# Six weight shifts moved from PSUM to SBUF, and another order of evictions and stores in the last step, in a fused attention and MoE kernel

## The chip, the cores and the metric

The kernel runs on one core of a Trainium2 chip. A core has five engines with an instruction queue each: TensorE (PE, matrix products into PSUM), VectorE (DVE), ScalarE (ACT), GpSimd (POOL) and SyncE (SP, which here issues every DMA). They run side by side and wait for each other through semaphores. SBUF is the working memory, PSUM the accumulation memory of eight banks that PE writes. The metric is the device time of one execution in microseconds; lower is better.

## The reference, cut to what matters

```python
def _attn_ref(q, k, v):                         # (4, 8, 768, 64)
    k_sum = k.reshape(B, H, nb, 32, D).max(axis=3)
    v_sum = v.reshape(B, H, nb, 32, D).mean(axis=3)
    scores_l = where(|i - j| < 16, scale * q @ k^T, -1e9)
    scores_s = scale * q @ k_sum^T + log(32)
    a = softmax(concat([scores_l, scores_s]))
    return a @ concat([v, v_sum])

def _moe_ref(x, w_in, w_out):                   # 3072 x 512, 512 x 2048, 2048 x 512
    h = x @ w_in
    return (h * cos(h)) @ w_out
```

The result of the attention, with its heads side by side, is the `x` of the second part. Everything is float32.

## The kernel before, in words

**Blocks, groups and steps.** The 3072 rows are done in eight blocks of 384. For each block four groups (a to d, two heads each) compute attention and leave the block's `x`, split into a high and a low part. Then, for each of 16 weight slices of 128 columns of `w_in` and 128 rows of `w_out`, a step forms `h`, its gate and the second product, which adds up in three PSUM banks, one for each chunk of 128 rows. Blocks 0 and 1 share the weights' loading: runs are block 0 with slices 0 to 5, block 1 with all 16, block 0 with slices 6 to 15 (its partial sums lie in DRAM meanwhile), and then blocks 2 to 7. There are 128 steps, `s0` to `s127`.

**The weights.** Each slice `w0` to `w15` is loaded in a raw form and turned into the values that PE multiplies, by a chain of operations on a tile of 128 x 1024: `ab` (`magnitude`, ACT, L388, into SBUF place `stage`), `cl` (`clamp`, L393, DVE or POOL, in place), `sh` (`shift`, DVE, L399), `lb` (`last_bits`, DVE, L407, in place), `fb` (`first_bits`, DVE, L415, into `stage` again), `hi` (copy to the high part, L350 on ACT or L352 on DVE) and `lo` (the rest, L356, on POOL or DVE). Where the shift's result goes is the token's argument: `w1.sh.6.7` is PSUM banks 6 and 7, through `work_in` and `two_banks`; the result also decides what L407 reads and writes and what L415 reads as its second operand, as their first operand is the raw slice in SBUF. The final weights of slice f live in an SBUF tile with the tag `w{f}`; the tiles `w8` to `w15` serve as raw and other room (`late0` to `late7`) before that.

**The order.** Each engine's queue follows one list written out by hand, `ORDER`: a token names who, what and with which arguments (`a0.nm` is the normalisation of group a of block 0; `.a`, `.v`, `.p` at the end is ACT, DVE or POOL). An engine takes its instructions strictly in this order. Around the shifts of slices 0 to 5, POOL has the softmax operations `su` (L593, subtract the maximum) and `nm` (L617, multiply by the inverse sum), the low parts `lo` and one clamp (`w3.cl.p`); DVE has the maxima (L588), sums (L609), inverses (L614) and the low parts of `x` (`xl`, L356) between them; PE the scores (L569), transposes (L626) and the values' product (L670).

**The last step.** `s127` adds the products of chunks 0 and 1 with the high part first (`dh`), then in `dl` the low-part products of chunks 0 and 1 and then all three of chunk 2. Then it evicts: `ta` and `tb` negate a bank into SBUF (`negative`, L806 on ACT, L808 on DVE), `st` and `sb` store. With no place named, `ta` takes the first half of a chunk and `tb` the second (`take_half`), in two halves of one tile, and each half is stored by itself (`store_half`, L830).

Of the kernel before, what the change touches and what calls it, by code (L numbers as in the profile page):

```python
# [10 lines left out]
F32 = mybir.dt.float32  # L11
F32R = mybir.dt.float32r
I32 = mybir.dt.int32
# [15 lines left out]
b0.ck.0.v a0.ck.0.a a0.ks.0 a0.ms.5.6 a0.ck.1.a a0.ks.1 b0.q a0.sc c0.tk.0.7 a0.z.1.a a0.z.0.v w1.l c0.ck.0.a a0.mx  # L29
d0.tk.0.1 c0.ks.0 a0.su c0.tq.0 c0.tk.1.3 d0.q c0.cq.a d0.tk.1.4 c0.ms.6.5 d0.ks.1 a0.ex v0_1.h.p c0.ks.1 c0.ck.1.v  # L30
w0.l d0.ks.0 c0.sc a0.sm c0.v c0.z.1.a v0_0.h.v b0.tq.7 c0.z.0.a b0.ms.0.3 b0.ck.1.a a0.iv v0_0.s.p b0.cq.a v0_1.s.v
d0.ck.0.a b0.sc w1.ab.0 c0.mx c0.m d0.tq.5 b0.z.1.a w1.cl.v c0.su d0.ms.2.1 b0.z.0.a w2.l w1.sh.6.7 d0.cq.a d0.ck.1.a
d0.sc w1.lb a0.nm c0.ex a0.v d0.z.1.a w1.fb.1 a0.tp.0.3 d0.z.0.a a0.tp.1.0 w0.ab.0 a0.m d0.mx w1.hi.a w0.cl.v d0.su
d0.m c0.sm w0.sh.4.5 w5.l w1.lo.p c0.iv w2.ab.0 w0.lb c1.m a0.cp.0.a w2.cl.v c0.nm d0.ex b1.q w0.fb.1 a0.cp.1.a w3.l
a0.va.1 d0.sm w0.hi.a d1.m w2.sh.6.7 w0.lo.p c0.tp.0.2 c1.q d0.iv w5.ab.0 w2.lb b1.tq.3 a1.q a0.xh.a d0.nm c0.tp.1.0
w2.fb.1 c0.cp.0.a d0.v c0.cp.1.a w5.cl.v w2.hi.a c0.va.2 a0.xl w2.lo.p d0.tp.0.6 c0.xh.a w5.sh.4.5 w4.l d0.tp.1.7 a1.m
b0.mx w3.ab.0 a1.tq.0 w5.lb b0.su a1.v a1.cq.a a1.ms.1.0 w5.fb.1 w3.cl.p b0.ex b0.m d0.cp.0.a a1.sc b0.sm b1.cq.a
c1.tq.6 d0.cp.1.a c0.xl a1.z.1.a d0.va.3 b0.iv w3.sh.4.5 b0.nm a1.z.0.a b1.m c1.ms.7.2 d0.xh.a a1.mx c1.cq.a d1.q
w4.ab.0 c1.sc w3.lb a1.su b0.v b0.tp.0.0 w5.hi.a b0.tp.1.1 d0.xl w4.cl.v c1.z.0.a c1.v b0.cp.0.a w4.sh.6.7 c1.z.1.a
b1.ms.3.0 b0.cp.1.a v1_0.l c1.mx a1.ex w8.l w4.lb c1.su b0.va.2 b1.sc a1.sm b0.xh.a w5.lo.p c1.ex d1.tq.1 b0.xl  # L40
b1.z.1.a a2.q a1.iv s0.up.2 w4.fb.0 b1.z.0.a a1.nm w3.fb.1 w4.hi.a a1.tp.0.0 d1.cq.a w4.lo.v w9.l d1.ms.3.6 s0.tu
a1.cp.0.a b1.v c1.sm w8.ab.0 a1.tp.1.7 d1.sc s0.re c1.iv a1.cp.1.a s1.up.4 w8.cl.v c1.nm w10.l s0.si b1.mx d1.v
# [130 lines left out]
s123.hi.a s124.si s123.lo.p s124.sq s124.ga s126.up.3 s124.hi.v s124.lo.v s127.up.4 s126.tu s125.tu s125.re s126.re  # L173
s123.dh s126.si s125.si s123.dl s125.sq s126.sq s124.dh s125.ga s125.hi.v s125.lo.v s124.dl s127.tu s125.dh s127.re
s126.ga s127.si s126.hi.v s127.sq s125.dl s126.lo.v s126.dh s127.ga s127.hi.a s126.dl s127.lo.p s127.dh s127.dl
s127.ta.2.a s127.ta.0.0.v s127.st.2 s127.tb.2.v s127.st.0 s127.ta.1.1.v s127.sb.2 s127.st.1
"""

BLOCK = 32
# [4 lines left out]
def tile_kernel(  # L184
# [20 lines left out]
    nc = tc.nc  # L205

    B, H, S, D = q.shape
    NT, DM = out.shape
    DF = w_in.shape[1]
    P = 128  # L210
# [6 lines left out]
    TB = S // 2  # L217
# [20 lines left out]
    xp = ctx.enter_context(tc.tile_pool(name="xp", bufs=1))  # L238
# [51 lines left out]
    for hh in range(2):  # L290
# [3 lines left out]
            out=rows, in_=rows, pattern=[[0, QC + 1], [1, W]], compare_op=ALU.is_ge,  # L294
# [3 lines left out]
            out=rows, in_=rows, pattern=[[0, QC + 1], [-1, W]], compare_op=ALU.is_ge,  # L298
# [28 lines left out]
    wp = ctx.enter_context(tc.tile_pool(name="wp", bufs=1))  # L327
# [15 lines left out]
    def two_banks(i):  # L343
        return banks[:, i : i + 2, :].rearrange("p b n -> p (b n)").bitcast(I32)
# [13 lines left out]
    def room_for(i):  # L358

        return stage.tile([P, 2 * DM], I32, name=f"stage{i}")  # L360

    class Slice:
# [16 lines left out]
        def work_in(self, where):  # L379
            if not where:  # L380
                return self.u
            return two_banks(where[0]) if len(where) == 2 else room_for(*where)

        def magnitude(self, i):
# [317 lines left out]
    class Step:  # L702
# [106 lines left out]


        def take_half(self, i, h, eng):
            if (i, 0) not in self.o:
                t = xp.tile([P, 2, TB], F32R, name="last", tag="xh0%d" % (self.blk % 2)).rearrange("p c n -> p (c n)")
                self.o[i, 0], self.o[i, 1] = (t[:, n * DM // 2 : (n + 1) * DM // 2].bitcast(F32) for n in range(2))
            self.negative(eng, self.o[i, h], self.acc[i][:, h * DM // 2 : (h + 1) * DM // 2])

        def take_rest(self, i, eng):
# [9 lines left out]

        def store_half(self, i, h):
            r0, c = self.blk * TB + i * P, slice(h * DM // 2, (h + 1) * DM // 2)
            nc.sync.dma_start(out=out[r0 : r0 + P, c], in_=self.o[i, h])  # L830

        def store_rest(self, i):
            self.store_half(i, 1)
# [124 lines left out]
```

## Time and profile before

| | us |
|---|---|
| median of 3 runs | 663.58 |
| the three runs | 661.78, 663.58, 663.86 |
| span of the profiled execution | 660.1 |
| busy in it: PE, DVE, ACT, POOL | 632.6, 449.7, 363.9, 221.8 |
| last instruction of PE ends | 655.1 |

The span goes from the first to the last instruction of one profiled execution; that execution's own total isn't given on the page, and the difference to the median of the runs, some 3.5 us, is what lies around the span. A line of a group reads: source line, engine, operation, what it writes and reads, shapes and count, then busy us, mean ns of one, and the idle time in front of it with what ended it. A line of the timeline reads: start, length, engine, line, operation, and in brackets the idle time in front of it. SPq is SP issuing a DMA. In the tiles' names `banks` is PSUM; `stage`, `late`, `w`, `sc`, `t` and `last` are SBUF.

### The profile page before, as it was taken

To read this page: it belongs to the slowest core of one execution; us is meant where nothing else is said; L and a number is where in the kernel's file an instruction comes from. 1 tells how busy PE (TensorE), PEld (TensorE's weight loads), DVE (VectorE), ACT (ScalarE), POOL (GpSimd) and SP (SyncE) were. 2 spreads that over 40 slices of the span, in tenths; PEclk is the share of its full clock that TensorE was granted. 3 is DMA by queue.
4 is the path that set the end of the run, shared out by engine and by line. 5 is a ranking of instruction groups with operands and counts; after the bars stand their busy time and mean duration, and the time that the engine had idled before them with its cause. 6 is when DMAs were issued, how large, how long until landed. Compare 5 with 4: busy or idle time off the path is not lost.

```text
span 660.1 us, 13282 instructions
## 1 busy us (share of the span) xinstructions
PE 632.6 (96%) x5141; PEld 560.2 (85%) x5141; DVE 449.7 (68%) x798; ACT 363.9 (55%) x640; POOL 221.8 (34%) x219
## 2 busy tenths in 40 slices
PE   6478999999999999999999999999999999999996
PEld 5256889989988998898898899889889989899985
DVE  4887999887855576668797777576876756433344
ACT  2656977776554485437477464356554645444342
POOL 4784896764430342301323411112330212010110
PEclk9869999999999999999999999999999999999999
DMA  9997906544243244525445433424364332000001
GB/s 224 259 271 203 276 15 223 169 109 71 55 122 85 91 124 132 127 59 114 111 107 135 147 98 97 114 43 85 115 163 104 92 94 70 5 1 17 16 17 48
DMA packets 167158, 72.68 MB, mean 110 GB/s; under 512 B 136824, under 2 KB 155832, under 8 KB 167096
## 3 DMA queue, kind: packets, MB, share of 16 engines
q1 hardware_dynamic: 167096, 71.84, 40.9%
q8 instruction: 40, 0.66, 0.4%
q14 instruction: 22, 0.18, 0.1%
HBM read 53.72 MB, written 15.73 MB: 105 GB/s over the span
## 4 chain that ended last, share of the span: by engine, by line
PE 86%; DMA 5%; SPq 3%; POOL 2%; DVE 1%; issue 1%; ACT 1%; DVEq 0%; POOLq 0%; ACTq 0%
PE banks L770 39%; PE banks L714 39%; PE banks L569 4%; PE banks L670 3%; DMA late<-in_moe_w_out_dram 3%; DMA late<-in_v_dram 1%; SPq L456 1%; POOL w L356 1%; DMA late<-in_q_dram 1%; POOL gl L356 1%; SPq L493 1%; POOL stage L393 0%; ACT stage L388 0%; PE banks L556 0%; DVE m L588 0%
## 5 line engine op out<-in xcount | busy, mean ns | idle before, releaser
L714 PE MATMUL banks<-xh,w 128*128 128x384 f32 x1024 | 272.1, 337 | 0.1
L770 PE MATMUL banks<-w,gh 128*128 128x512 f32 x768 | 198.1, 393 | 0.2 <-ACT gh L350 0.2
L714 PEld LDWEIGHTS banks<-xh,w 128*128 128x128 f32 x1024 | 185.9, 188 | 2.8 <-ACT pt L350 0.4
L714 PE MATMUL banks<-xl,w 128*128 128x384 f32 x512 | 171.4, 335 | 0.0
L770 PEld LDWEIGHTS banks<-w,gh 128*128 128x128 f32 x768 | 142.6, 188 | 29.0 <-ACT gh L350 0.5
L724 ACT ACTIVATE t<-banks 128x384 int32<-128x384 f32 x128 | 62.5, 489 | 133.6 <-DVE gl L356 54.9
L356 POOL TENSOR_TENSOR gl<-t,gh 128x384 fp32r<-128x384 f32 x55 | 56.6, 1029 | 221.4 <-ACT gh L350 86.0
L770 PE MATMUL banks<-w,gl 128*128 128x512 f32 x384 | 109.8, 394 | 0.1
L727 DVE SCALAR_TENSOR_TENSOR t<-t,banks 128x384 f32<-128x384 int32 x128 | 70.0, 548 | 56.9 <-ACT t L724 56.2
L732 ACT ACTIVATE t<-t 128x384 f32<-128x384 f32 x128 | 66.7, 523 | 66.3 <-DVE t L727 66.0
L714 PEld LDWEIGHTS banks<-xl,w 128*128 128x128 f32 x512 | 96.1, 188 | 1.6
L739 DVE SCALAR_TENSOR_TENSOR t<-t,banks 128x384 f32<-128x384 f32 x128 | 69.3, 546 | 41.2 <-ACT t L735 41.0
L770 PEld LDWEIGHTS banks<-w,gl 128*128 128x128 f32 x384 | 71.1, 188 | 14.6 <-DVE gl L356 0.2
L593 POOL TENSOR_TENSOR sc<-sc,m 128x720 f32<-128x720 f32 x28 | 40.1, 1431 | 129.2 <-DVE m L588 129.2
L735 ACT ACTIVATE t<-t 128x384 f32<-128x384 f32 x128 | 65.8, 521 | 2.1
L617 POOL TENSOR_TENSOR sc<-sc,r 128x720 f32<-128x720 f32 x28 | 39.5, 1411 | 51.4 <-DVE r L614 50.3
L350 ACT CAST gh<-t 128x384 fp32r<-128x384 f32 x68 | 34.7, 510 | 33.2 <-PE banks L770 16.5
L356 DVE TENSOR_TENSOR gl<-t,gh 128x384 fp32r<-128x384 f32 x73 | 41.7, 572 | 12.6 <-ACT gh L350 6.5
L356 POOL TENSOR_TENSOR w<-stage,w 128x1024 fp32r<-128x1024 f32 x15 | 36.2, 2416 | 10.0 <-ACT w L350 8.6
L352 DVE CAST gh<-t 128x384 fp32r<-128x384 f32 x60 | 23.2, 386 | 22.2 <-PE banks L770 20.4
L580 DVE SCALAR_TENSOR_TENSOR sc<-banks,mask 128x360 f32<-128x360 f32 x48 | 24.4, 524 | 19.2 <-PE banks L569 19.0
L569 PEld LDWEIGHTS banks<-kd,qd 64*64 64x64 f32 x1344 | 28.4, 135 | 9.4 <-issue 6.7
(102 smaller groups left out, 620.7 us busy)
## 6 DMA issues: line engine op xcount, KB each, us to landing
pd<-stage SPq DMA_DIRECT2D x22, 384.0 KB
late<-in_moe_w_in_dram SPq DMA_DIRECT2D x16, 512.0 KB
late<-in_moe_w_out_dram SPq DMA_DIRECT2D x16, 512.0 KB
pt<-pd SPq DMA_DIRECT2D x66, 96.0 KB
vn<-in_v_dram SPq DMA_DIRECT2D x52, 120.0 KB
out_dram<-stage SPq DMA_DIRECT2D x23, 256.0 KB
kn<-in_v_dram SPq DMA_DIRECT2D x24, 192.0 KB
qn<-in_q_dram SPq DMA_DIRECT2D x92, 48.0 KB
```

The costliest lines, as they stand in the source:

```text
L350: eng.copy(out=out, in_=in_)
L356: eng.tensor_tensor(out=lo, in0=src, in1=hi.bitcast(F32), op=ALU.subtract)
L569: nc.tensor.matmul(out=self.sp[hh][s * QT : (s + 1) * QT, c, lo : lo + n], lhsT=self.qd[rows, t * QT : (t + 1) * QT], rhs=self.kd[rows, ke ...
L593: nc.gpsimd.tensor_tensor(out=self.sc, in0=self.sc, in1=self.m.unsqueeze(2).broadcast_to([P, U, NK]), op=ALU.subtract)
L617: nc.gpsimd.tensor_tensor(out=self.sc, in0=self.sc, in1=self.r.unsqueeze(2).broadcast_to([P, U, NK]), op=ALU.mult)
L714: nc.tensor.matmul(out=self.h, lhsT=w_of(name, self.f)[:, c * P : (c + 1) * P], rhs=x_of(self.blk, part, c), start=n == 0, stop=n == last,)
L724: nc.scalar.activation(out=self.t.bitcast(I32), in_=self.h, func=AF.Copy, scale=1.0 / TWO_PI)
L727: nc.vector.scalar_tensor_tensor(out=self.t, in0=self.t.bitcast(I32), scalar=-TWO_PI, in1=self.h, op0=ALU.mult, op1=ALU.add)
L732: nc.scalar.activation(out=self.t, in_=self.t, func=AF.Sin, scale=0.5)
L735: nc.scalar.activation(out=self.t, in_=self.t, func=AF.Square, scale=math.sqrt(2.0))
L739: nc.vector.scalar_tensor_tensor(out=self.t, in0=self.t, scalar=-1.0, in1=self.h, op0=ALU.add, op1=ALU.mult)
L770: nc.tensor.matmul(out=self.acc[i], lhsT=g[:, i * P : (i + 1) * P], rhs=w_of(name, self.f), start=self.first and n == 0, stop=self.last an ...
```

## The change

In `ORDER` the six tokens `w1.sh.6.7`, `w0.sh.4.5`, `w2.sh.6.7`, `w5.sh.4.5`, `w3.sh.4.5` and `w4.sh.6.7` become `w1.sh.8`, `w0.sh.8`, and so on, at the same places; nothing else in the list moves up to the last line. The argument 8 makes `work_in` take an SBUF tile with the tag of the slice's own final weights. Slices 6 to 15 keep their banks.

The last line of `ORDER` is another: chunk 0 is evicted by DVE and stored, then chunk 1 by ACT (before: by DVE, last) and stored, then chunk 2 in halves, the first by DVE and the second by ACT (before: the first by ACT, the second by DVE, chunk 2 ahead of chunk 1). The halves get tiles of their own, and the second one's store is issued by ACT's queue.

```diff
-d0.ck.0.a ... w2.l w1.sh.6.7 d0.cq.a d0.ck.1.a
+d0.ck.0.a ... w2.l w1.sh.8 d0.cq.a d0.ck.1.a
...
-s127.ta.2.a s127.ta.0.0.v s127.st.2 s127.tb.2.v s127.st.0 s127.ta.1.1.v s127.sb.2 s127.st.1
+s127.ta.0.0.v s127.st.0 s127.ta.1.1.a s127.st.1 s127.ta.2.v s127.tb.2.a s127.st.2 s127.sb.2
...
         def work_in(self, where):
             if not where:
                 return self.u
+            if where == (8,):
+                return wp.tile([P, 4 * DM], I32, name=f"u{self.f}", tag=f"w{self.f}")[:, : 2 * DM]
             return two_banks(where[0]) if len(where) == 2 else room_for(*where)
...
         def take_half(self, i, h, eng):
-            if (i, 0) not in self.o:
-                t = xp.tile([P, 2, TB], F32R, name="last", tag="xh0%d" % (self.blk % 2)).rearrange("p c n -> p (c n)")
-                self.o[i, 0], self.o[i, 1] = (t[:, n * DM // 2 : (n + 1) * DM // 2].bitcast(F32) for n in range(2))
+            t = xp.tile([P, 2, TB], F32R, name="last", tag="x%s0%d" % ("hl"[h], self.blk % 2))
+            self.o[i, h] = t.rearrange("p c n -> p (c n)")[:, : DM // 2].bitcast(F32)
             self.negative(eng, self.o[i, h], self.acc[i][:, h * DM // 2 : (h + 1) * DM // 2])
...
         def store_half(self, i, h):
             r0, c = self.blk * TB + i * P, slice(h * DM // 2, (h + 1) * DM // 2)
-            nc.sync.dma_start(out=out[r0 : r0 + P, c], in_=self.o[i, h])
+            (nc.sync, nc.scalar)[h].dma_start(out=out[r0 : r0 + P, c], in_=self.o[i, h])
```

More of the change, by code (lines that the diff above doesn't have):

```diff
@@ L31 @@
 w0.l d0.ks.0 c0.sc a0.sm c0.v c0.z.1.a v0_0.h.v b0.tq.7 c0.z.0.a b0.ms.0.3 b0.ck.1.a a0.iv v0_0.s.p b0.cq.a v0_1.s.v
-d0.ck.0.a b0.sc w1.ab.0 c0.mx c0.m d0.tq.5 b0.z.1.a w1.cl.v c0.su d0.ms.2.1 b0.z.0.a w2.l w1.sh.6.7 d0.cq.a d0.ck.1.a
+d0.ck.0.a b0.sc w1.ab.0 c0.mx c0.m d0.tq.5 b0.z.1.a w1.cl.v c0.su d0.ms.2.1 b0.z.0.a w2.l w1.sh.8 d0.cq.a d0.ck.1.a
 d0.sc w1.lb a0.nm c0.ex a0.v d0.z.1.a w1.fb.1 a0.tp.0.3 d0.z.0.a a0.tp.1.0 w0.ab.0 a0.m d0.mx w1.hi.a w0.cl.v d0.su
-d0.m c0.sm w0.sh.4.5 w5.l w1.lo.p c0.iv w2.ab.0 w0.lb c1.m a0.cp.0.a w2.cl.v c0.nm d0.ex b1.q w0.fb.1 a0.cp.1.a w3.l
-a0.va.1 d0.sm w0.hi.a d1.m w2.sh.6.7 w0.lo.p c0.tp.0.2 c1.q d0.iv w5.ab.0 w2.lb b1.tq.3 a1.q a0.xh.a d0.nm c0.tp.1.0
-w2.fb.1 c0.cp.0.a d0.v c0.cp.1.a w5.cl.v w2.hi.a c0.va.2 a0.xl w2.lo.p d0.tp.0.6 c0.xh.a w5.sh.4.5 w4.l d0.tp.1.7 a1.m
+d0.m c0.sm w0.sh.8 w5.l w1.lo.p c0.iv w2.ab.0 w0.lb c1.m a0.cp.0.a w2.cl.v c0.nm d0.ex b1.q w0.fb.1 a0.cp.1.a w3.l
+a0.va.1 d0.sm w0.hi.a d1.m w2.sh.8 w0.lo.p c0.tp.0.2 c1.q d0.iv w5.ab.0 w2.lb b1.tq.3 a1.q a0.xh.a d0.nm c0.tp.1.0
+w2.fb.1 c0.cp.0.a d0.v c0.cp.1.a w5.cl.v w2.hi.a c0.va.2 a0.xl w2.lo.p d0.tp.0.6 c0.xh.a w5.sh.8 w4.l d0.tp.1.7 a1.m
 b0.mx w3.ab.0 a1.tq.0 w5.lb b0.su a1.v a1.cq.a a1.ms.1.0 w5.fb.1 w3.cl.p b0.ex b0.m d0.cp.0.a a1.sc b0.sm b1.cq.a
-c1.tq.6 d0.cp.1.a c0.xl a1.z.1.a d0.va.3 b0.iv w3.sh.4.5 b0.nm a1.z.0.a b1.m c1.ms.7.2 d0.xh.a a1.mx c1.cq.a d1.q
-w4.ab.0 c1.sc w3.lb a1.su b0.v b0.tp.0.0 w5.hi.a b0.tp.1.1 d0.xl w4.cl.v c1.z.0.a c1.v b0.cp.0.a w4.sh.6.7 c1.z.1.a
+c1.tq.6 d0.cp.1.a c0.xl a1.z.1.a d0.va.3 b0.iv w3.sh.8 b0.nm a1.z.0.a b1.m c1.ms.7.2 d0.xh.a a1.mx c1.cq.a d1.q
+w4.ab.0 c1.sc w3.lb a1.su b0.v b0.tp.0.0 w5.hi.a b0.tp.1.1 d0.xl w4.cl.v c1.z.0.a c1.v b0.cp.0.a w4.sh.8 c1.z.1.a
 b1.ms.3.0 b0.cp.1.a v1_0.l c1.mx a1.ex w8.l w4.lb c1.su b0.va.2 b1.sc a1.sm b0.xh.a w5.lo.p c1.ex d1.tq.1 b0.xl
```

## The prediction

> **What bounds the kernel now.** I read the page first (its head, and a group that is needed further down: busy us and mean ns of one stand behind the bar), then the table of stretches.
>
> ```profile
> span 660.1 us, 13282 instructions
> ...
> L356 DVE TENSOR_TENSOR gl<-t,gh 128x384 fp32r<-128x384 f32 x73 | 41.7, 572 | 12.6 <-ACT gh L350 6.5
> ```
>
> ```profile
> 22.80:62.30 39.50, 26.21 (x360) 19.66 (x359) 34.85 (x41) 26.06 (x46) 28.02 (x16) 0.78 0.80 218
> ```
>
> ```profile
> 120.00:640.00 520.00, 520.00 (x4108) 466.87 (x4107) 341.75 (x645) 279.59 (x495) 135.34 (x123) 1.00 0.35 89
> ```
>
> The columns of a stretch are its length, then busy us of PE, PEld, DVE, ACT and POOL, then the granted clock, the DMA share and GB/s. From 120 to 640 us PE is busy without a gap: nothing outside PE can shorten that part, and nothing that PE loses earlier is won back there. All of PE's idle time is at the two ends, and the change touches just these. In the first, 22.8 to 62.3 us, where slices 0 to 5 are prepared, PE is busy 26.2 of 39.5 us, DVE 34.9 and POOL 28.0. So whatever delays the DVE and POOL chains here by more than their slack delays PE and the end. How much slack is there, and where?
>
> ```profile
> 56.71 0.92 PE L670 MATMUL banks<-pt,vn 120*64 120x64 f32 x24 [2.27 <-DMA vn<-in_v_dram]
> ```
>
> ```profile
> 59.30 1.39 POOL L617 TENSOR_TENSOR sc<-sc,r 128x720 f32<-128x720 f32 x1
> ```
>
> ```profile
> 60.89 0.53 PEld L626 LDWEIGHTS banks<-ident,sc 128*120 128x120 f32 x4
> ```
>
> These are rows of the timeline (start, length, instruction). At 56.71 PE waited 2.27 us for a load of v (group b of block 0), so up to there a faster DVE wins nothing, and a late one has about two microseconds to spend. Behind it the slack is gone: POOL's normalisation of group a of block 1 runs 59.30 to 60.69, and PE's transposes of its result (60.89) follow 0.2 us behind it. PE is in order; if that POOL instruction is late, PE is.
>
> **The change, part 1: six shifts.** Each slice makes three DVE instructions: the shift (L399), L407 and L415. The first two write PSUM now, the last two read their second operand from it. After the change all three read and write SBUF alone. Nothing is added to any queue and no order changes. The groups of that stretch (count, then busy us, mean ns):
>
> ```profile
> L407 DVE SCALAR_TENSOR_TENSOR banks<-late,banks 128x1024 int32<-128x1024 int32 x6 | 7.3, 1224 | 0.0
> L399 DVE TENSOR_SCALAR banks<-stage 128x1024 int32<-128x1024 int32 x6 | 7.3, 1221 | 1.4 <-POOL stage L393 0.7 <-ACT late L350 0.6
> L415 DVE SCALAR_TENSOR_TENSOR stage<-late,banks 128x1024 int32<-128x1024 int32 x6 | 7.2, 1210 | 0.5 <-POOL w L356 0.3
> ...
> L593 POOL TENSOR_TENSOR late<-late,m 128x720 f32<-128x720 f32 x3 | 4.9, 1644 | 6.2 <-DVE m L588 6.2
> ...
> L393 DVE TENSOR_SCALAR stage<-stage 128x1024 f32<-128x1024 f32 x5 | 3.7, 742 | 0.4 <-ACT stage L388 0.3
> ...
> L617 POOL TENSOR_TENSOR late<-late,r 128x720 f32<-128x720 f32 x2 | 3.2, 1616 | 0.0
> ...
> L356 DVE TENSOR_TENSOR w<-stage,w 128x1024 fp32r<-128x1024 f32 x1 | 1.2, 1226 | 0.0
> ```
>
> The gain: no row shows the shift from SBUF to SBUF. The nearest is L393, the same operation type and size there: 0.69 us undisturbed (0.70 below). Upper bound is today's 1.22. I take 0.69, which frees 6 x 0.53 = 3.2 us of DVE, and the wait of 0.6 us for ACT to clear a bank goes too. L407 and L415 stay at 1.2 us, since L356, two SBUF operands of the same size, takes 1.23.
>
> The cost: what two SBUF operands do beside POOL. Rows from DVE's timeline, then POOL's at the same times:
>
> ```profile
> 22.93 0.70 DVE L393 TENSOR_SCALAR stage<-stage 128x1024 f32<-128x1024 f32 x1 [0.31 <-ACT stage L388]
> ...
> 47.83 1.23 DVE L399 TENSOR_SCALAR banks<-stage 128x1024 int32<-128x1024 int32 x1 [0.65 <-POOL stage L393]
> ...
> 329.56 1.10 DVE L356 TENSOR_TENSOR gl<-t,gh 128x384 fp32r<-128x384 f32 x1
> ```
>
> ```profile
> 23.09 1.78 POOL L593 TENSOR_TENSOR late<-late,m 128x720 f32<-128x720 f32 x1
> ...
> 47.77 1.39 POOL L617 TENSOR_TENSOR sc<-sc,r 128x720 f32<-128x720 f32 x1
> ...
> 328.86 1.39 POOL L593 TENSOR_TENSOR sc<-sc,m 128x720 f32<-128x720 f32 x1 [3.77 <-DVE m L588]
> ```
>
> At 47.8 a shift into PSUM lies wholly beside a POOL instruction: both keep their lengths, 1.23 and 1.39. At 329.56 a subtraction with both inputs in SBUF (0.57 us on average over the kernel, by its group above) meets a POOL instruction that runs until 330.25; it ends at 330.66, so it did nothing until 0.16 us before POOL's end. At 22.93 DVE came first, with a one-input SBUF to SBUF instruction, and POOL's 1.39 became 1.78: it ended 0.39 us late, just the time by which DVE ran on, less 0.15. So such a DVE instruction and a POOL instruction exclude each other for their whole length, save 0.15 us at each change of hands.
>
> The Trainium skill has this as a rule, in "SBUF — State Buffer", section "Who interferes with whom": VectorE's second port pair belongs to GpSimd too and is locked, not shared, by an instruction in a two-port mode or with two SBUF inputs against a GpSimd one that reads SBUF. The rows above agree for a tensor_tensor and a tensor_scalar; no row here has a scalar_tensor_tensor with two SBUF inputs. By that rule the sum is the one that follows; by the rows alone it could also be that of rival 1.
>
> After the change 18 more DVE instructions are of that kind: 6 x 0.69 + 7.3 + 7.2 = 18.6 us. With those that are already (five L393 at 0.69, 3.5 us; L356, 1.2) DVE needs 23.3 us of exclusive time, and POOL 28.0 less 1.2 us of such waits that are in its lengths already (three L593 of 1.64 and two L617 of 1.62, against 1.39 alone), 26.8. Together 50.1 us in a stretch of 39.5. Some 24 changes of hands give back 24 x 0.15 = 3.6. The stretch cannot be done in under 46.5 us: **at least 7.0 us late**, even if one of the two were always ready. They aren't always. I laid the DVE and POOL queues out instruction by instruction in their order, with lengths from these rows, ACT, PE and the loads between them as traced, and exclusion as above. Laid out so, the kernel of before reaches its row at 56.71 within 0.1 us. The changed one: slice 0's L407 is ready at 32.3, waits for slice 1's low part on POOL and ends at 35.7 (32.1 before); POOL's clamp of slice 3 starts at 52.0, not 44.2; the product at 56.71 starts at 63.2; the normalisation at 59.30 starts at 68.6 and ends at 70.9, not 60.7, since it waits for slice 4's L415. From 64 us on PE is late by 9.3 to 10.1 us and stays **9.4 us late**. PE's few gaps between 64 and 100 us end with a result of ACT, DVE or POOL and move along, and its work afterwards is unbroken. The 3.2 us of DVE freed by the faster shift are in this already.
>
> Bounds of this term: if the shift stays at 1.22 us and excludes nobody, the same layout gives 7.7; if it runs at 0.69 and excludes nobody, 6.4; if it takes 1.22 and still excludes POOL, 12.5. More idle PE may hold the granted clock (0.78 over the stretch) lower for longer; in the layout PE waits for the other two anyway, so I count at worst 1 us for it, an estimate. If exclusion doesn't touch L407 and L415 at all, the term is 0.
>
> **Part 2: the last step.**
>
> ```profile
> 653.82 0.62 PE L770 MATMUL banks<-w,gl 128*128 128x512 f32 x2
> ...
> 654.25 0.69 DVE L808 TENSOR_SCALAR stage<-banks 128x512 f32<-128x512 f32 x1 [3.02 <-PE banks L770]
> ...
> 655.16 0.38 ACT L806 ACTIVATE last<-banks 128x256 f32<-128x256 f32 x1 [3.32 <-PE banks L770]
> 655.57 0.33 SPq L830 DMA_DIRECT2D out_dram<-last  x1
> 655.57 0.42 DVE L808 TENSOR_SCALAR last<-banks 128x256 f32<-128x256 f32 x1 [0.63 <-ACT last L806]
> ...
> 656.96 0.41 SPq L826 DMA_DIRECT2D out_dram<-stage  x1
> ```
>
> ```profile
> L806 ACT ACTIVATE stage<-banks 128x512 f32<-128x512 f32 x10 | 5.9, 593 | 4.1 <-PE banks L770 2.6 <-DMA out_dram<-stage 1.4
> ```
>
> ```profile
> 657.00:657.25 0.25, 0.00 (x0) 0.00 (x0) 0.00 (x0) 0.00 (x0) 0.00 (x0) 1.00 1.05 385
> ```
>
> The last two fences are ACT's group for a whole chunk, and a stretch among the stores, whose last column is GB/s. Before, the first of four stores is issued at 655.57 and the last at 656.96, because DVE evicts the second chunk last. Its products end at 654.44 (the first row: the last products of chunks 0 and 1). After: chunk 0 leaves DVE at 654.94, and SP, with nothing ahead of it, issues its store from 654.96 to 655.34. ACT, idle for 3.3 us, takes chunk 1 from 654.48 for 0.59 us, to 655.07; SP's issue is 655.44 to 655.82. The halves of chunk 2 start together at 655.16, as the 0.63 us wait for a shared place is gone, and end by 655.58; ACT issues one store at about 655.56, behind which nothing is queued on ACT, SP the other at 655.92. The last issue comes 1.04 us earlier, the first 0.6. Four issues at 0.46 us each took 1.4 us before, the 768 KB take 2.0 us at 385 GB/s: if the transfers ran without a gap before, only the first issue's 0.6 counts; if they waited for issues, up to 1.04 does. The first store is the larger one now, so gaps go; I take nearer to the second. **Part 2 gives -0.9 us.** Bounds: -1.1 and, as no row has a store issued by ACT, +0.5; I take 0.4 us for that issue, like SP's here, and it has about 0.5 to spare before it would be last.
>
> **Sum.** 9.4 - 0.9 = +8.5 us on a span of 660.1. The median of 663.58 holds some 3.5 us around a span of this length (the profiled run's own total isn't on the page); I leave them as they are: 672.1, put at **672.0 us**.
>
> **The rivals.**
> 1. *The sharing doesn't touch these instructions* (the other side: not slower). Its one mechanism: L407 and L415, the operation with a scalar and two tensors, keep clear of POOL although both inputs are in SBUF, because exclusion needs a tensor_tensor. Then DVE gains 3.2 us up to 56.7, where PE waits 2.27 us for v anyway, so nothing reaches the end, and part 2 leaves 663.58 - 0.9 = 662.7. For it: no row shows that operation with two SBUF inputs. Against: the subtraction at L356 needs just the same reads. It decides if POOL keeps 1.39 and 2.36 us beside L407 and L415. 12%.
> 2. *The same, and DVE's gain arrives*: if loads issued earlier let PE start sooner by half of the 2.27 us, -1.1 - 0.9 gives 661.5. Against: DVE waits for ACT and POOL several times before 56.7. 3%.
> 3. *The shift excludes nobody*, only L407 and L415 do: 6.4 to 7.7 less 0.9, 669 to 670.4. For it: no row has a shift inside SBUF. 15%.
> 4. *Exclusion costs more*, because DVE keeps the port from one of its instructions to the next or the granted clock stays low: 12.5 - 0.9, 675. 10%.
> That the shift stays in PSUM after all can't be: the new place is an SBUF tile of that slice's own. Nor does the tile's reuse by the final weights add a wait; their writer waits for L415's result anyway.
>
> **How the numbers follow.** The forecast itself has 60%, cases 3 and 4 the next 25%, all of them slower: 85%. Case 1 lies within 0.3% (2.0 us, about what a measurement can tell from no change): 12%; case 2 is faster by more than that: 3%. The range of the slower cases goes from the floor of 7.0 less 0.9, and 2 us of slack won back, at 667.5, to case 4 with an us of clock, at 676.5; it holds about 80% and leaves out cases 1 and 2.
>
> **What would show it.** Right: L407 and L415 of slices 0 to 5 in a mean of 1.8 us or more, or POOL's L593, L617 and L356 lengthened in 22.8 to 72 us; the product at 56.71 after 61; the shift at 0.69 when alone; the last issue by 656.96 + 9.4 - 1.0 on the profile's scale. Wrong: L407 at 1.22 beside POOL's unchanged 1.39 (case 1), or lengthened rows while PE's 56.71 hasn't moved, which would mean more slack in the loads than I see.

## The result, and the profile after

| | before | after |
|---|---|---|
| median of four runs, us | 662.90 | 670.27 |
| all runs, us | 661.78, 662.23, 663.58, 663.86 | 669.94, 670.24, 670.30, 670.79 |
| ratio after to before | | 1.0118 (95%: 1.0100 to 1.0136) |
| span of the profiled execution, us | 660.1 | 668.5 |
| end of PE's last product | 655.12 | 664.25 |
| from there to the end of the span | 4.98 | 4.25 |

The change costs 7.4 us by the medians and 8.4 us by the two spans. The last two rows split the spans: the start-up loses 9.13 us, the last step wins 0.73. PE's last product before is this row of its timeline:

```profile
654.73 0.39 PE L770 MATMUL banks<-w,gl 128*128 128x512 f32 x1
```

The code behind the edit moved down by two lines: L399, L407, L415, L593, L617, L670 are now L401, L409, L417, L595, L619, L672; L356 is the same. In the last step L770, L806 and L808 are now L772, L808 and L810, and the stores L826 and L830 are L827 and L831.

The table of stretches of the changed kernel (length, busy us of PE, PEld, DVE, ACT, POOL, granted clock, DMA share, GB/s):

```profile
22.80:62.30 39.50, 24.30 (x289) 16.95 (x289) 37.02 (x33) 21.63 (x37) 27.56 (x12) 0.65 0.79 220
...
120.00:640.00 520.00, 520.00 (x4111) 467.19 (x4110) 345.26 (x646) 280.39 (x495) 139.88 (x129) 1.00 0.36 93
```

The middle is as full as before. In the first stretch DVE is busier (37.0 us against 34.9) and yet has done only 33 instructions in place of 41, and PE has done 289 products in place of 360. DVE's "busy" time is longer because its instructions are. Their groups from 22.8 to 72 us, by which time the six slices are done:

```profile
L409 DVE SCALAR_TENSOR_TENSOR u<-late,u 128x1024 int32<-128x1024 int32 x6 | 12.7, 2121 | 0.0
L417 DVE SCALAR_TENSOR_TENSOR stage<-late,u 128x1024 int32<-128x1024 int32 x6 | 12.6, 2114 | 0.2
L356 POOL TENSOR_TENSOR w<-stage,w 128x1024 fp32r<-128x1024 f32 x4 | 10.4, 2598 | 5.1 <-ACT w L350 5.1
L401 DVE TENSOR_SCALAR u<-stage 128x1024 int32<-128x1024 int32 x6 | 6.7, 1124 | 2.2 <-POOL stage L395 2.1
...
L619 POOL TENSOR_TENSOR sc<-sc,r 128x720 f32<-128x720 f32 x3 | 5.6, 1867 | 0.0
```

L409 and L417 take 2.12 and 2.11 us in place of 1.22 and 1.21, and POOL's L619 1.87 in place of 1.39 when alone. The wait doesn't show as idle time in front of an instruction (0.0, 0.2 us): the engine has begun and is held inside it. Two shifts of DVE's timeline show that the shift itself is of this kind too:

```profile
24.31 1.76 DVE L401 TENSOR_SCALAR u<-stage 128x1024 int32<-128x1024 int32 x1
...
38.77 0.68 DVE L401 TENSOR_SCALAR u<-stage 128x1024 int32<-128x1024 int32 x1
```

Where POOL is idle when it starts (38.77), it takes 0.68 us; the one at 24.31 meets an L619 of POOL that ends at 25.52, and ends 0.55 us after it. The product that started at 56.71 before comes at 61.62, and the costliest place is behind it, in the timeline of all engines:

```profile
61.62 0.92 PE L672 MATMUL banks<-pt,vn 120*64 120x64 f32 x24
...
65.36 2.40 POOL L356 TENSOR_TENSOR w<-stage,w 128x1024 fp32r<-128x1024 f32 x1
...
65.45 5.72 DVE L417 SCALAR_TENSOR_TENSOR stage<-late,u 128x1024 int32<-128x1024 int32 x2
...
67.71 2.38 POOL L619 TENSOR_TENSOR sc<-sc,r 128x720 f32<-128x720 f32 x1
...
70.15 1.11 PE L628 MATMUL banks<-ident,sc 128*120 128x128 f32 x4 [2.29 <-POOL sc L619]
```

Two L417 of 1.21 us take 5.72 us together, since each waits for a whole POOL instruction, and POOL's L619, which waits for the first of them, ends at 70.09. PE's transposes and the loads of their weights follow at 70.15, 9.26 us after the loads' 60.89 of before, with 2.29 us of idle time that names POOL. From there PE's delay stays: 9.13 us at its last product.

The end of the span, from the timeline:

```profile
663.86 0.39 PE L772 MATMUL banks<-w,gl 128*128 128x512 f32 x1
664.10 0.81 SPq L827 DMA_DIRECT2D out_dram<-stage  x2
664.28 0.42 DVE L810 TENSOR_SCALAR last<-banks 128x256 f32<-128x256 f32 x1 [0.22 <-PE banks L772]
664.74 0.38 ACT L808 ACTIVATE last<-banks 128x256 f32<-128x256 f32 x1 [0.54 <-DVE last L810]
665.00 0.40 SPq L831 DMA_DIRECT2D out_dram<-last  x1
665.16 0.37 ACTq L831 DMA_DIRECT2D out_dram<-last  x1
```

Against the end of PE's last product (664.25) the first store is issued 0.60 us earlier than before (-0.15 in place of +0.45) and the last 0.93 us earlier (+0.91 in place of +1.84).

### The profile page after: what moved, and what is told of

The parts are those of the page before. It is cut to its first block, busy times and chain, and to the rows that moved or that the text cites. A ratio compares the mean times of both kernels' runs of the same rounds, so it can differ in the third digit from the quotient of the medians.

```text
span 668.5 us, 13279 instructions
## 1 busy us (share of the span) xinstructions
PE 637.3 (95%) x5141; PEld 563.4 (84%) x5141; DVE 460.9 (69%) x797; ACT 364.8 (55%) x641; POOL 228.2 (34%) x219
## 4 chain that ended last, share of the span: by engine, by line
PE 85%; POOL 4%; DMA 3%; DVE 2%; SPq 2%; issue 2%; ACT 1%; POOLq 0%; DVEq 0%
PE banks L716 39%; PE banks L772 39%; PE banks L571 4%; PE banks L672 3%; DMA late<-in_moe_w_out_dram 2%; DMA late<-in_v_dram 1%; SPq L458 1%; POOL stage L395 1%; POOL w L356 1%; DVE u L409 1%; POOL sc L619 1%; PE banks L628 1%; DVE stage L417 1%; POOL late L595 0%; POOL late L259 0%
## 5 line engine op out<-in xcount | busy, mean ns | idle before, releaser
L772 PE MATMUL banks<-w,gh 128*128 128x512 f32 x768 | 198.1, 393 | 0.0
L772 PEld LDWEIGHTS banks<-w,gh 128*128 128x128 f32 x768 | 142.6, 188 | 28.6
L356 POOL TENSOR_TENSOR gl<-t,gh 128x384 fp32r<-128x384 f32 x55 | 56.6, 1029 | 222.2 <-ACT gh L350 86.0
L772 PE MATMUL banks<-w,gl 128*128 128x512 f32 x384 | 109.8, 394 | 0.1
L595 POOL TENSOR_TENSOR sc<-sc,m 128x720 f32<-128x720 f32 x28 | 41.9, 1495 | 126.4 <-DVE m L590 124.9
L772 PEld LDWEIGHTS banks<-w,gl 128*128 128x128 f32 x384 | 71.1, 188 | 14.6 <-DVE gl L356 0.2
L619 POOL TENSOR_TENSOR sc<-sc,r 128x720 f32<-128x720 f32 x28 | 40.9, 1462 | 51.4 <-DVE r L616 50.3
L356 DVE TENSOR_TENSOR gl<-t,gh 128x384 fp32r<-128x384 f32 x73 | 41.6, 571 | 12.6 <-ACT gh L350 6.5
L356 POOL TENSOR_TENSOR w<-stage,w 128x1024 fp32r<-128x1024 f32 x15 | 37.2, 2483 | 12.2 <-ACT w L350 10.8
```

The source lines that it names most:

```text
L356: eng.tensor_tensor(out=lo, in0=src, in1=hi.bitcast(F32), op=ALU.subtract)
L595: nc.gpsimd.tensor_tensor(out=self.sc, in0=self.sc, in1=self.m.unsqueeze(2).broadcast_to([P, U, NK]), op=ALU.subtract)
L619: nc.gpsimd.tensor_tensor(out=self.sc, in0=self.sc, in1=self.r.unsqueeze(2).broadcast_to([P, U, NK]), op=ALU.mult)
L772: nc.tensor.matmul(out=self.acc[i], lhsT=g[:, i * P : (i + 1) * P], rhs=w_of(name, self.f), start=self.first and n == 0, stop=self.last an ...
```

## The experiments

The theory: DVE instructions whose inputs are all in SBUF and POOL instructions that read SBUF exclude each other, and the start-up has no room for that. The rivals: the loss has another cause (new tiles and their waits, later loads, the clock); only some of the three DVE instructions exclude; the last step has a part in it. Medians stand beside those of the kernel before on the same chip.

**The two parts by themselves.** Each is the kernel before with one half of the diff (the tokens `w0.sh.8` to `w5.sh.8` with `work_in`, or the last line of `ORDER` with `take_half` and `store_half`).

> Only the six shifts are moved to SBUF, the last step is that of before. Theory: POOL and DVE exclude each other, PE's last product ends 9.1 us later, +9.1 us on the median (8.5 to 10). Rival (the two parts act on each other, or the last step costs): +7.4 or less.

Measured: 671.70 against 662.56, ratio 1.0145 (1.0128 to 1.0162), +9.1 us; PE's last product ends at 664.40 in its profile.

> Only the last step is changed, the shifts stay in PSUM. Theory (the loss is all in the start-up, the last step is a small gain): start-up as before, PE's last product ends at 655.1 as before, from there to the end of the span 4.2 us in place of 5.0, so -0.7 us on the median. Rival (the store from ACT's queue lands later, or the order of chunks costs): +0.3 to +0.5 us. Rival (part of the +8.4 comes from the last step): +1 us or more.

Measured: 661.92 against 662.56, ratio 0.9992 (0.9978 to 1.0006): no difference that the runs can tell. In its profile the last product ends at 656.92 and the span at 661.2, so 4.28 us in place of 4.98. All of the loss is part 1's, and part 2 is a gain of 0.7 us that only the profile shows. The two medians add up to +8.5 us, so the parts don't act on each other by more than the runs can tell. The 12 runs of part 2 alone go from 659.88 to 664.34, and in its profile PE's last product came 1.8 us later than in that of before although nothing in its start-up is changed: single executions differ by that much there.

**POOL emptied.** The decisive pair: in both runs the low parts and one clamp go to DVE and POOL's two softmax operations get shorter; the second has the shifts in SBUF besides.

```diff
-... w1.lo.p ... w0.lo.p ... w2.lo.p ... w3.cl.p ... w5.lo.p ... w3.lo.p ...
+... w1.lo.v ... w0.lo.v ... w2.lo.v ... w3.cl.v ... w5.lo.v ... w3.lo.v ...
...
         def less_max(self):
+            n = 4 if self.blk < 2 else NK
             nc.gpsimd.tensor_tensor(
-                out=self.sc, in0=self.sc, in1=self.m.unsqueeze(2).broadcast_to([P, U, NK]), op=ALU.subtract
+                out=self.sc[:, :, :n], in0=self.sc[:, :, :n], in1=self.m.unsqueeze(2).broadcast_to([P, U, n]), op=ALU.subtract
```

> The kernel of before, with POOL emptied in the start-up: the low parts of slices 0, 1, 2, 3, 5 and the clamp of slice 3 go from POOL to DVE at the same places of the list, and in blocks 0 and 1 POOL's two softmax operations work on 4 of 120 columns only (the rest of that arithmetic is left out). Base for the next run. Layout of the queues: the product at 56.71 where it was, the end within 1 us of before (+0.3).

> The same emptied POOL (same part left out), and the six shifts in SBUF. Theory (the loss is POOL and DVE excluding each other): with nothing on POOL there is no loss, so within 1 us of the run before it (layout 0.0), L409 and L417 at 1.2 us and L401 at 0.7. Rival (the loss has another cause: the new tiles and their waits, loads that come later, the clock, DVE itself): again 7 to 9 us slower than the run before it.

Measured: 662.58 with the shifts in PSUM and 662.31 with them in SBUF (before: 662.88; ratios 0.9992, 0.9980 to 1.0004, and 0.9990, 0.9975 to 1.0005). The groups of the second, 22 to 72 us:

```profile
L409 DVE SCALAR_TENSOR_TENSOR u<-late,u 128x1024 int32<-128x1024 int32 x6 | 7.2, 1204 | 0.0
...
L401 DVE TENSOR_SCALAR u<-stage 128x1024 int32<-128x1024 int32 x6 | 4.1, 680 | 0.1
```

The tiles and the shifts are those of the changed kernel and DVE has the low parts to do as well, yet without POOL's work L409 is back at 1.20 us, the shift runs at 0.68, and the 9 us are gone. So the new tiles, their waits and the loads aren't the cause. The granted clock of 22.8 to 62.3 us is 0.74 in both runs; in the changed kernel it is 0.65 (0.78 before). A share of the lower clock in the 9 us wasn't measured by itself, but PE's transposes at 70.15 wait 2.29 us for POOL, so what sets their start is not PE's own speed. The faster shift wins nothing either: 3.2 us less of DVE moves the end by no more than the runs can tell.

**Which instructions exclude.** The token of L407 takes a place as well, so the data can change sides in the middle of the chain.

```diff
-... w1.sh.6.7 ... w1.lb ...
+... w1.sh.8 ... w1.lb.6.7 ...
```

(and so for all six slices; the other run has `w1.sh.6.7` and `w1.lb.8`)

> Shift of slices 0 to 5 to SBUF, L407 reads it there and writes the two PSUM banks, L415 reads PSUM as before; last step of before. Theory (both inputs in SBUF is what excludes, wherever the result goes): shift and L407 exclude POOL, L415 doesn't; L407 lengthened, L415 at 1.21; the end +5.3 us. Rival (an instruction must read and write SBUF only): L407 at 1.22, only the shift excludes, +1 us or less.

> Shift of slices 0 to 5 to PSUM as before, L407 reads PSUM and writes SBUF, L415 has both inputs in SBUF; last step of before. Theory: only L415 excludes POOL: L407 at 1.22, L415 lengthened; the end +1.7 us by the layout, which came out 1.5 us short in the two runs of three slices, so up to +3.2. Rival (a third of the loss for a third of the instructions): +3. Rival (no exclusion by L415): 0.

Measured: 667.30 and 664.60 against 662.88; ratios 1.0058 (1.0037 to 1.0079) and 1.0021 (1.0008 to 1.0033); +4.4 and +1.7 us (5.3, and 1.7 to 3.2, were expected). The clock of 22.8 to 62.3 us is 0.78 in the first, as before, so the loss doesn't need a lower one. The groups of the first run, then of the second:

```profile
L409 DVE SCALAR_TENSOR_TENSOR banks<-late,u 128x1024 int32<-128x1024 int32 x6 | 12.7, 2123 | 0.1
L417 DVE SCALAR_TENSOR_TENSOR stage<-late,banks 128x1024 int32<-128x1024 int32 x6 | 7.3, 1211 | 1.4 <-POOL w L356 1.2
```

```profile
L417 DVE SCALAR_TENSOR_TENSOR stage<-late,u 128x1024 int32<-128x1024 int32 x6 | 11.8, 1978 | 0.5 <-POOL w L356 0.3
...
L409 DVE SCALAR_TENSOR_TENSOR u<-late,banks 128x1024 int32<-128x1024 int32 x6 | 7.3, 1216 | 0.0
```

L409 with both tensors in SBUF is held (2.12 us) though its result goes to PSUM; with one in PSUM it isn't (1.22) though its result goes to SBUF. The inputs decide.

**The disputed cost by itself.** A program of its own: eight equal DVE instructions start beside six equal POOL instructions.

```python
def meet(dve, pool_op):
    ...
    for n in range(max(NV, NP)):
        if n < NP:
            pool_op()
        if n < NV:
            dve()
```

> Another program (none of the reference's arithmetic, its output is a constant): nine times, eight equal DVE instructions start together with six equal POOL instructions, on operands of the kernel's sizes. Theory (a DVE instruction whose inputs are all in SBUF, faster than 1 us or with two tensors, excludes a POOL instruction that reads SBUF): shift SBUF to SBUF, and the operation with two tensors with both in SBUF, whether its result goes to SBUF or to PSUM: both engines take turns, DVE's mean 1.7 to 2.8 us and POOL's 1.9 to 2.8. Shift SBUF to PSUM, the same operation with one tensor in PSUM (result in PSUM or SBUF), the sum or maximum along a row: DVE 1.22, 1.22, 1.21, 0.9 and POOL 1.39 each. POOL's clamp takes turns too (4.6 us); POOL's memset reads nothing and doesn't (DVE 1.21). Rival (what counts is that the instruction writes SBUF): shift to PSUM and L407 to PSUM free, L415 with a tensor in PSUM and result in SBUF excludes. Rival (any two SBUF accesses of the two engines get in each other's way): all nine lengthen.

Its groups, DVE's first. L113 and L116 are the shift to SBUF and to PSUM; L119, L122, L125 and L128 the operation with two tensors (two in SBUF; one in PSUM, twice; two in SBUF, result in PSUM); L131 a maximum along rows. Their partners on POOL are, in the same order, L86, L89, L92, L95, L98, L101 and L104. L134 met POOL's clamp (L107), L137 its memset (L110).

```profile
L128 DVE SCALAR_TENSOR_TENSOR banks<-raw,a 128x1024 int32<-128x1024 int32 x8 | 16.2, 2028 | 0.9 <-ACT raw L74 0.6
L119 DVE SCALAR_TENSOR_TENSOR d<-raw,d 128x1024 int32<-128x1024 int32 x8 | 16.2, 2027 | 0.8 <-ACT d L75 0.6
L113 DVE TENSOR_SCALAR d<-a 128x1024 int32<-128x1024 int32 x8 | 11.9, 1493 | 0.8 <-ACT d L75 0.6
L134 DVE SCALAR_TENSOR_TENSOR d<-raw,d 128x1024 int32<-128x1024 int32 x8 | 11.9, 1493 | 3.4 <-ACT d L75 3.1
L122 DVE SCALAR_TENSOR_TENSOR banks<-raw,banks 128x1024 int32<-128x1024 int32 x8 | 9.8, 1229 | 0.9 <-ACT raw L74 0.6
L116 DVE TENSOR_SCALAR banks<-a 128x1024 int32<-128x1024 int32 x8 | 9.8, 1228 | 0.8 <-ACT a L73 0.5
L137 DVE SCALAR_TENSOR_TENSOR d<-raw,d 128x1024 int32<-128x1024 int32 x8 | 9.8, 1226 | 13.8 <-ACT d L75 13.5
L125 DVE SCALAR_TENSOR_TENSOR d<-raw,banks 128x1024 int32<-128x1024 int32 x8 | 9.8, 1221 | 0.8 <-ACT d L75 0.6
L131 DVE TENSOR_REDUCE r<-zz 128x6 f32<-128x720 f32 x8 | 7.2, 902 | 0.2
```

```profile
L107 POOL TENSOR_SCALAR big<-big 128x1024 f32<-128x1024 f32 x6 | 24.1, 4024 | 1.5 <-ACT m L78 1.1
L92 POOL TENSOR_TENSOR s<-s,m 128x720 f32<-128x720 f32 x6 | 13.3, 2222 | 2.1 <-ACT m L78 1.7
L101 POOL TENSOR_TENSOR s<-s,m 128x720 f32<-128x720 f32 x6 | 13.2, 2206 | 2.4 <-ACT m L78 2.0
L86 POOL TENSOR_TENSOR s<-s,m 128x720 f32<-128x720 f32 x6 | 10.2, 1698 | 10.3 <-ACT m L78 9.9
L89 POOL TENSOR_TENSOR s<-s,m 128x720 f32<-128x720 f32 x6 | 8.3, 1389 | 2.8 <-ACT m L78 2.4
```

L89's 1.39 us is POOL's undisturbed length, and its partner L116 keeps 1.23. The pairs with all of DVE's inputs in SBUF lengthen on both sides (2.03 with 2.22, 1.49 with 1.70); those with one input in PSUM, the maximum (0.90 with 1.39) and the memset do not. In the trace the two engines take strict turns, 2.33 us for one L119 and one L92, where 1.22 + 1.39 would be 2.61: each change of hands saves 0.14. The mean of L113, 1.49, falls below the 1.7 expected because its first and its last were not held (0.69 each, the six between them 1.76); its partner's 1.70 is below the 1.9 expected. The clamp came out otherwise than expected: three times a DVE instruction met its beginning and was held for 0.72 us and not for the 3.62 of the clamp; later ones beside the same clamp ran at 1.23.

The Trainium skill, "SBUF — State Buffer", section "Who interferes with whom", says that a DVE instruction with two SBUF inputs contends with a GpSimd one that reads SBUF, not with one that only writes, and that the two-port modes contend too. These runs agree for the two inputs (2.03 us beside a tensor_tensor of POOL, 1.23 beside its memset). The shift within SBUF, held as well, agrees with the second statement if its 0.69 us, against 1.23 into PSUM, comes from such a mode, which no row names. What the Trainium skill says on the same page in section "SBUF: two separate sides", that whichever starts first gets the pair for the whole instruction, agrees for POOL's tensor_tensor, not for the clamp (0.72 of 3.62 us).

**Half of the slices.** The tokens of three slices each.

> Shifts of slices 0, 1 and 2 in SBUF, those of 3, 4, 5 in PSUM, last step of before. Theory (exclusion, laid out queue by queue, with 2.3 us of slack at PE's wait for v): product at 56.71 later by 3.6 us, the end by +3.0 us. Rival (a price per slice, without slack): half of 9.1, +4.5 us. Rival (only the last slices matter, since PE waits for v anyway): 0.

> Shifts of slices 3, 4 and 5 in SBUF, those of 0, 1, 2 in PSUM, last step of before. Theory (same layout): product at 56.71 not later, the transposes at 60.89 later by 3.3 us, the end by +2.6 us; together with the run of slices 0 to 2 that is less than the 9.1 of all six, as the slack is used up once only. Rival (a price per slice): +4.5 us.

Measured: 667.13 and 666.57 against 662.56; ratios 1.0069 (1.0055 to 1.0084) and 1.0059 (1.0044 to 1.0074); +4.6 and +4.0 us, where the layout had 3.0 and 2.6. Rows of PE's timeline, of the first run and then of the second:

```profile
60.06 0.92 PE L672 MATMUL banks<-pt,vn 120*64 120x64 f32 x24
...
66.26 0.65 PE L628 MATMUL banks<-ident,sc 128*120 128x128 f32 x4 [0.86 <-POOL sc L619]
```

```profile
56.26 0.92 PE L672 MATMUL banks<-pt,vn 120*64 120x64 f32 x24
...
64.65 0.65 PE L628 MATMUL banks<-ident,sc 128*120 128x128 f32 x4 [2.29 <-POOL sc L619]
```

Up to here the layout held: the product of 56.71 comes 3.4 us later with slices 0 to 2 (3.6 expected) and not later with 3 to 5, and the transposes of 60.89 are 5.4 and 3.8 us late (3.3 expected in the second). Behind that the layout let PE win some of it back, 0.7 us in the second run, to end at +3.0 and +2.6. In the two profiles PE's last product ends 5.5 and 3.4 us late, so PE won back nothing in the first and 0.4 us in the second. The two losses add up to 8.6 of the 9.1 us of all six, so a price per slice describes the totals better than the slack did.

**The last step.** Two edits on the run with the new last step alone. First, chunk 2 in halves by rows:

```diff
-            self.o[i, h] = t.rearrange("p c n -> p (c n)")[:, : DM // 2].bitcast(F32)
-            self.negative(eng, self.o[i, h], self.acc[i][:, h * DM // 2 : (h + 1) * DM // 2])
+            self.o[i, h] = t.rearrange("p c n -> p (c n)")[h * P // 2 : (h + 1) * P // 2, :DM].bitcast(F32)
+            self.negative(eng, self.o[i, h], self.acc[i][h * P // 2 : (h + 1) * P // 2, :])
```

> The shifts of before and the new last step, with chunk 2 halved by rows (64 partitions of 512 columns each) and not by columns. In the changed kernel ACT's half started only at 664.74, when DVE's half was done (664.70), though the two have places of their own. Theory (the wait is for the PSUM bank, which both halves read, in the same partitions): on other partitions ACT starts within 0.1 us of DVE, DVE's half takes 0.69 and ACT's 0.6 us. Rival (the order is kept for any two readers of a bank, or because of the tile's name): ACT starts when DVE ends, 0.69 us later.

```profile
655.90 0.68 DVE L810 TENSOR_SCALAR last<-banks 64x512 f32<-64x512 f32 x1 [0.21 <-PE banks L772]
656.62 0.59 ACT L808 ACTIVATE last<-banks 64x512 f32<-64x512 f32 x1 [0.80 <-DVE last L810]
```

ACT still starts when DVE has ended (656.58), on other partitions and with a place of its own. From PE's last product to the end of the span it is 4.7 us, in place of 4.28. This is a single run (662.39 us), so its time decides nothing.

Second, PE's products chunk by chunk, and then the same with two names for the halves' places:

```diff
         def early(self):
-            chunks = range(NTT - 1 if self.g == len(steps) - 1 else NTT)
+            chunks = range(1 if self.g == len(steps) - 1 else NTT)
```

> The shifts of before and the new last step, and in the last step's products PE does chunk 0 with both parts first, then chunk 1, then chunk 2. Theory (first store's issue sets the start of the transfers, 768 KB at 385 GB/s follow): DVE evicts chunk 0 about 0.5 us earlier against PE's last product, its store is issued 0.65 us before that product's end in place of 0.15, and from the last product to the end of the span 3.8 us in place of 4.25; median 0.4 us under the run with the new last step alone, 1.0 under before. Rival (the last store's issue and its way to DRAM set the end): 4.2 us as without it.

> The run with the chunks in order again, with one edit: the two places of chunk 2's halves have different names. If the name kept the second half waiting (it was the same for both), ACT's half starts with DVE's, 0.45 us earlier, and the last product to the end of the span takes 3.5 us in place of 3.8. If it is the bank, as with the halves by rows, nothing changes there. The whole: if the start-up differs between programs only by chance, 1.0 to 1.3 us under before; if the 2.5 us of the run with the chunks in order are its own, again 2 us or more.

Measured: 659.81 against 662.32, ratio 0.9969 (0.9958 to 0.9980), and 661.55 against 662.71, ratio 0.9976 (0.9962 to 0.9990). The timeline of the first:

```profile
652.86 0.69 DVE L810 TENSOR_SCALAR stage<-banks 128x512 f32<-128x512 f32 x1 [2.57 <-PE banks L772]
...
653.58 0.92 SPq L827 DMA_DIRECT2D out_dram<-stage  x2
...
653.80 0.39 PE L772 MATMUL banks<-w,gl 128*128 128x512 f32 x1
```

The first store is issued 0.61 us ahead of the last product's end (654.19), and the span ends 3.81 us after it, as expected (3.8), and 3.82 in the run with two names, whose ACT half waits as before: the name has no part in it. The last store is issued 0.91 us behind the last product's end, just as in the run with the new last step alone, where the span ends 4.28 us behind it. So the 0.47 us between the two come with the earlier issues, not with the last one. Both runs are faster than the kernel before; the last step accounts for 1.2 us of it (4.98 before). The rest of the first run's 2.5 us lies in the start-up (its product of 56.71 starts at 54.78), which the edit doesn't touch, and the second run with the same order shows 1.2. So the 1.2 is shown and the rest of the first run's gain is open; the start-up's spread between executions is of that size.

## Why the prediction was right

- *The mechanism*: right. The 18 DVE instructions and POOL exclude each other, wait and gain at a change of hands included (0.15 predicted, 0.14 measured). Emptying POOL takes the loss away, and the program of its own shows the exclusion without the rest of the kernel. The floor of 7.0 us was less safe than it was called: it counts all 3.62 us of the clamp as exclusive, and with the 0.72 measured it would be 4.1, an estimate. The forecast went by the layout and not by the floor.
- *L407 and L415*: right, 2.12 and 2.11 us, "a mean of 1.8 us or more" predicted. Rivals 1 and 2 (they keep clear of POOL) fall. *The shift*: right, 0.68 alone and held beside POOL, so rival 3 falls. Rival 4 (exclusion costs more) falls with the loss itself, 9.1 us and not 12.5, and with the strict turns of the program of its own.
- *The size of part 1*: 9.4 predicted; 9.13 by the profiles, 9.1 by the run with part 1 alone. That it came out so close is in part luck. The normalisation was to end at 70.9, 10.2 us late, of which PE was to win back 0.8; it ended at 70.09, and of the 9.26 us at the transposes PE won back only 0.13. The two errors nearly cancel.
- *The product of 56.71*: at 61.62, not 63.2. The layout had POOL's clamp of slice 3 exclude DVE for its whole length, which the program of its own refutes, and this execution began the stretch 0.4 us (DVE) to 0.75 us (POOL) earlier; how the 1.6 us divide between the two wasn't tried. In the changed kernel's trace no DVE instruction is held by the clamp: the L417 at 50.13 goes ahead of it, and the clamp takes 4.59 us in place of 3.62. The transposes behind it are set by POOL and L417, where the layout was 0.8 us late.
- *The work behind 61 us*: wrong for three slices at a time. The layout's catching up between 61 and 72 us didn't happen (+4.6 and +4.0, not 3.0 and 2.6). Why PE doesn't catch up is open. With all six the layout let it win back 0.8 us at most, so the forecast hardly suffered.
- *Part 2*: -0.73 us by the profiles, -0.9 predicted, first and last issue 0.60 and 0.93 us earlier (0.6 and 1.04 predicted), and ACT's issue took 0.37 (0.4). The prediction took the gain nearer to that of the last issue; 0.73 lies nearer to the first's, and the products chunk by chunk win 0.47 us more with the last issue unmoved. One step is wrong: "The halves of chunk 2 start together at 655.16, as the 0.63 us wait for a shared place is gone". The place is gone and the wait is still there, with halves of columns (0.54 us), of rows (0.80), and with names of their own (0.54). What the halves still share is the PSUM bank, and by the profile the instruction waits for a semaphore of DVE's, which the program sets. Chunks 0 and 1, in banks of their own, do overlap. That it is the bank is what is left, not shown by a run in which the halves lie in two banks; nor does any run show whether the chip would hold ACT without that semaphore. The Trainium skill, "PSUM — Partial Sum Buffer", section "PSUM bank collisions raise a hardware error", tells of a dependency that the compiler's scheduler adds between two engines on one bank and the same 32 partitions, readers too; here an order stands also between halves on different partitions (DVE ends at 656.58, ACT starts at 656.62).
- *The time*: 672.0 predicted, 670.27 measured. The sum was right (+8.5; 8.4 between the two spans; 7.4 between the medians, whose interval of +6.6 to +9.0 holds it) and the base was too high. The prediction put 3.5 us around the profiled execution of before. In every later run the total is 1.8 us above the span (670.3 and 668.5), so that execution took about 661.9, one of the fastest, and the median of before with one more run is 662.90 and not 663.58.

## What to carry to other kernels

Before a DVE operand moves from PSUM to SBUF, add up the time in which DVE has all its inputs in SBUF and the time in which POOL reads SBUF, in the stretch where both are busy: here the sum was longer than the stretch, and the loss came out at the end, whatever the instruction itself gained. A sum that fits is no all-clear: with L415 alone within SBUF the same sum is some 38.7 us in the stretch of 39.5 (26.8 for POOL, 11.9 for DVE, an estimate from the prediction's rows), and the end still came 1.7 us later: PE's transposes wait 1.79 us for a POOL instruction in that run's profile. An instruction that is held this way shows as a longer busy time with no idle time in front of it, so look at its mean beside its length alone. At the end of a kernel, try an order of the last products that completes the first chunk early: here the stores issued earlier moved the end by as much, with the last issue where it was.

## What the runs showed of the hardware that was not expected

In the program of its own, POOL's tensor_scalar of 128 x 1024 (3.62 us) kept DVE off for 0.72 us only, while its tensor_tensor kept it off to within 0.14 us of its end. After a DVE instruction that was held, POOL's next one, if it is ready, goes ahead of DVE's next one: the engines alternate one by one (2.33 us a pair), so two short DVE instructions in a row can wait for two long ones of POOL, as the 5.72 us at 65.45 show.
